# Token numbers from a turned table, a branch moved up with hints, and scatters without an order

## The chip, the cores and the metric

The kernel runs on one core of a Trainium2 chip. A core has a matrix engine (PE, with its weight loads PEld), a vector engine (DVE), an activation engine (ACT), a general engine (POOL, which also issues indirect DMAs), a sync engine (SP, which issues most other DMAs), and 16 DMA engines. Each engine runs its own instruction stream in order; semaphores tie the streams together. The metric is device microseconds of one execution; lower is better.

## The reference, cut to what matters

Three layers follow one another. The first is retention attention over 8 batches, 8 heads, 576 positions and 64 dimensions: scores `q @ k^T / 8`, multiplied by a decay `gamma ** (i - j)` for `i >= j` and 0 otherwise, then multiplied by `v`. Its output is laid out as 4608 tokens of 512 numbers.

The second is a mixture of experts: each token goes to one of 8 experts, the one with the largest gate logit, and becomes `gate_w * (relu(x @ w1[e]) @ w2[e])` with `w1[e]` of 512 x 1024. Which tokens an expert gets is known only while the kernel runs.

The third is a dense layer for all tokens: `h = relu(x @ w_in)` and `(h * h) @ w_out`, with 2048 hidden columns. The output is 4608 rows of 512 numbers in the order of the tokens.

## The kernel before, in words

**Phase 0** computes the attention in 36 tiles of 128 tokens, the gate, and each token's place in a table. The table has 288 columns (36 for each expert) of 128 rows, and holds token numbers: the tokens of one expert fill its columns one after another. It is made by matmuls in one PSUM bank (`tps`), and `tab_out` (line 252) writes it as whole numbers into `tab`, 128 partitions by 288 columns. The token rows lie in DRAM as `xd`.

**Phases 1 and 2** (`phase12`, line 676) run the experts over slots of 512 tokens. The slots in order are `"E"`, then 0 to `NF` = 8; slot `NF` has 256 tokens. Every slot has 8 units `(s, f)`, so the main loop counts `i` from 0 to 79, and slot `NF` is `i` = 72 to 79. In step `i` the code issues `first` of the next unit (12 matmuls, then `hh` on ACT and `hl` on DVE) and `second` of this one (12 matmuls), then splits a piece of a later expert's weights into a high and a low part (`wsplit`: ACT writes the high part, DVE the low one) and loads another from DRAM (`wload`, line 404). Beside it `convs` turns the weights of the third layer into the form that phase 3 wants and stores them in DRAM as `wc`, and `combos` does the same for the first tile's inputs.

A slot's tokens are gathered by `gather` (line 429): POOL copies 4 columns of `tab` into `ix` and fetches the rows of `xd` that they name. At the slot's end `second` stores the results as `yd` (line 847) and the slot's token numbers as `sd` (line 848). The tile `ix` holds a token number in each of 128 partitions, so this store of 2 KB writes 512 single numbers of 4 bytes:

```
sp.dma_start(so.rearrange("(j p) -> p j", p=P), ix[:, :wd // P])
```

If the tokens need more slots than there are, `extra` (line 916) runs them inside `tc.If(ext > x)`, nested for up to 7 more; `ext` is read at run time, and in these inputs the body isn't run. The branch stands in every engine's stream, and behind it each engine waits on its own semaphores. `extras` (line 935) is called at `u == (NF, 4)`, that is `i` = 76.

Four pairs of loads of third-layer weights (`wload2`, line 1022, whose DMAs are of line 1026, 8 in all, 896 KB each) are issued on SP: the pair `(0, 0)` and the pair `(0, 1)` at `i` = 73, the pair `(0, 2)` at `i` = 77, and the pair `(1, 0)` at `i` = 79.

**Phase 3** (`phase3`, line 1101) runs the third layer by 7-product block multiplication over 9 tiles of 512 tokens in 3 passes over the hidden columns. Its first tile needs all 12 loads of the first pass: the 8 above and 4 more of line 1143. The order of its instructions is written by a planner (`Plan`, line 1034): each operation is added with its engines, a guessed duration, keys read and written, and a time to land; `emit` works out due times backwards through the dependencies and then lists the operations by earliest start, ties by due time. In the last pass each tile ends with 4 indirect DMAs on POOL (line 1291), which scatter 128 rows each into `out`, at the token numbers `ixs` that were read back from `sd`. All of them write the key `("out",)`, so the planner, and the waits in the program, put each behind the one before.

Of the kernel before, what the change touches and what calls it, by code (L numbers as in the profile page):

```python
# [9 lines left out]
F32 = mybir.dt.float32  # L10
F32R = mybir.dt.float32r
BF16 = mybir.dt.bfloat16
I32 = mybir.dt.int32
U32 = mybir.dt.uint32
AF = mybir.ActivationFunctionType
ALU = mybir.AluOpType
AX = mybir.AxisListType
# [7 lines left out]
P = 128  # L25
NTILE = NT // P
TS = 512
NF = 8
# [5 lines left out]
KEYS = NE * DMAX  # L34
MAGIC = 12582912.0
IDOFF = float(NT // 2)
# [54 lines left out]
def kernel(ctx, tc, qT, kT, kN, vN, modT, w_gate, mbias, w1, w2, w_in, w_out,  # L91
# [32 lines left out]
    ring = [psX]  # L124

    xd = dram.tile([NT, DM], F32, name="xd")
    yd = dram.tile([DM, NT + TS], F32, name="yd")
    sd = dram.tile([NT + TS], I32, name="sd")
    wc = dram.tile([2, NFP, 2, P, 7 * 256], F32, name="wc")
    pd = dram.tile([9, P, 4 * DM], F32, name="pd")  # L130
    xc = dram.tile([9, 7, P, 4 * 256], F32, name="xc")
# [119 lines left out]

    def tab_out():
        dve.tensor_scalar(out=tab, in0=tps, scalar1=IDOFF, scalar2=None, op0=ALU.add)

    def count(t, name):
        ps = ring[0].tile([P, NE], F32, tag="g", name=name)
# [419 lines left out]
    def phase12():  # L676
        ring[0] = psG
        with ExitStack() as c1:
# [144 lines left out]
            def second(u, cols=range(KD)):  # L823
                s, f = u
                wd = width(s)
                hh, hl = HS.pop(u)
                w = W[s, f // 2][1]
                for c in cols:
                    if f == 0:
                        Y[s, c] = new(psY, [P, TS], F32, f"y{c}", f"y{c}")  # L830
                    cs = slice(c * P, c * P + P)
                    three(Y[s, c][:, :wd], (w[:, 0, f % 2, cs], w[:, 1, f % 2, cs]), (hh, hl), f == 0, f == 7)
                if f == 7:
                    if 0 in cols:
                        YE[s] = new(rp, [P, KD, TS], F32, "raw", "ye")
                    ye = YE[s]
                    for c in cols:
                        act.activation(ye[:, c, :wd], Y[s, c][:, :wd], AF.Copy)
                    if 3 not in cols:
                        return  # L840
                    ix = XG[s][1]
                    if s == "E":
                        yo, so = yd[:, 0:TS], sd[0:TS]
                    else:
                        reg = sp.value_load(slots[0:1, 2, s:s + 1], min_val=0, max_val=NT)
                        yo, so = yd[:, bass.ds(reg, wd)], sd[bass.ds(reg, wd)]
                    sp.dma_start(yo.rearrange("(c p) t -> p c t", p=P), ye[:, :, :wd])
                    sp.dma_start(so.rearrange("(j p) -> p j", p=P), ix[:, :wd // P])

            seq = ["E"] + list(range(NF + 1))  # L850
            us = [(s, f) for s in seq for f in range(8)]
# [62 lines left out]
                    yield  # L914

            def extra(x):
                with tc.If(ext > x):  # L917
                    s_ = NF + 1 + x
                    expert(s_)
                    gather(s_)  # L920
# [41 lines left out]
            for i, u in enumerate(us):  # L962
# [12 lines left out]
                        trans(nx, f - 3)  # L975
                if u == (NF, 7):
                    wload2(1, 0, wp)
                second(u)
                if s == "E" and f == 6:
                    trans(nx, 2)  # L980
# [3 lines left out]
                if i == 0:  # L984
                    for _ in route_a(last):
                        pass
                    next(cs)
                elif i == 1:
                    tb = table()
                    next(tb)  # L990
                    for _ in route_b(last, dve):
                        next(tb)
                elif i == 2:
                    ws(6, 2, 7)
                    tab_out()
                    for _ in range(10):
                        next(tb)
                elif i == 3:
                    for _ in tb:
                        pass  # L1000
                    ws(8, 2, 11)
                else:
                    wl(i + 9)
                    fill(wsg(i + 6, 2 if i < 10 else 1, i + 9), part(cs, 2250))
                    if i >= 68:
                        run(ex, 3)
                    if i == 73:
                        assert next(cs, 0) == 0 and next(ex, 0) == 0
                        wload2(0, 0, cv)
                if u == (NF, 1):  # L1010
                    wload2(0, 1, wp)
                if u == (NF, 4):
                    extras()
                if u == (NF, 5):
                    wload2(0, 2, wp)
                if i == 6:
# [84 lines left out]
    def phase3():  # L1101
        with ExitStack() as c2:
# [10 lines left out]
            xt = sb("xt", [P, 2, 256], F32)  # L1113
            OE = [sb("oe", [P, 4, DM], F32), yr]
            ixs = [sb(f"ix{j}", [P, 4], I32) for j in range(2)]
            BX, BY, BZ = banks[5:7], [banks[7], banks[4]], banks[0]
            BR = {c: banks[1 + "XYZ".index(c)].rearrange("p (b d) -> p b d", b=2) for c in "XYZ"}

# [131 lines left out]
            def hsplit(u, z, h, a, b, kz_):  # L1250
# [5 lines left out]
                                                          in1=h[:, 0, a:b].bitcast(F32), op=ALU.subtract),  # L1256
                         rs + ks[0], ks[1])

            def two(n, x):
                p, t = T3[n]  # L1260
                ends = p == len(PASSES) - 1
# [24 lines left out]
                if x in (4, 3):  # L1286
                    j0 = 2 if x == 4 else 0
                    kk = [("o", v, y) for y in ((4, 7) if x == 4 else (1, 6))]
                    if ends:
                        for j in (j0, j0 + 1):  # L1290
                            plan.add([(POOL_, 1.0)], lambda e, j=j: e.indirect_dma_start(  # L1291
                                out=out[:, :],
                                out_offset=bass.IndirectOffsetOnAxis(ap=ixs[n % 2][:, j:j + 1], axis=0),
                                in_=oe[:, j, :], in_offset=None), kk + [("ix", n % 2)], [("out",)], 4.2)
                    elif T3[n + 1][1] != t:
                        dma(pd[t, :, j0 * DM:j0 * DM + 2 * DM], oe[:, j0:j0 + 2].rearrange("p j d -> p (j d)"),
                            512, kk, [("pd", t, j0)])
# [77 lines left out]
```

## Time and profile before

| what | value |
| --- | --- |
| time, median of 3 runs (lowest to highest) | 1387.73 us (1386.54 to 1390.43) |
| the profiled execution: its time, its span | 1390.15 us, 1387.9 us |
| mean granted TensorE clock | 0.988 of full speed |
| PE busy (share of the span) | 1336.8 us (96%) |
| DVE, ACT, POOL busy | 1023.7, 628.2, 128.9 us |
| DMA | 332.43 MB, mean 240 GB/s |

The profile comes from one execution; all times in it are counted from the start of its span. A busy PE is one that has an instruction in its pipeline. In a view by stretches, `PEclk` is the granted clock of TensorE as a share of full speed and `DMA` the mean busy share of the 16 DMA engines, in which a packet counts from its start to its end, so that waiting packets count too. "Waits" tells which engine and line waited for which.

### The profile page before, as it was taken

How to read it: one execution, taken by the hardware profiler on the slowest of the kernel's cores; microseconds unless marked ns; L12 is line 12 of the kernel's file. 1: busy time of each engine (PE TensorE's matmuls, PEld its weight loads, DVE VectorE, ACT ScalarE, POOL GpSimd, SP SyncE). 2: the span in 40 equal slices, each digit the busy share in tenths (PEclk: the TensorE clock that was granted, in tenths of full speed). 3: DMA queues.
4: the chain of work that ended last, by engine and by line, in shares of the span. 5: the costliest groups of instructions: out<-in, count | busy, mean ns of one | idle time of the engine just before them, and what ended most of it. 6: DMA issues, size and time to landing. Idle time of an engine off the chain costs nothing. (4 is left out here: it accounts for less than half of the span.)

```text
span 1387.9 us, 26914 instructions
## 1 busy us (share of the span) xinstructions
PE 1336.8 (96%) x10640; PEld 1231.3 (89%) x10640; DVE 1023.7 (74%) x2084; ACT 628.2 (45%) x1265; POOL 128.9 (9%) x134
## 2 busy tenths in 40 slices
PE   6999999999999999988899999999999999999995
PEld 6888877888878888877899999999999999999995
DVE  2787867877878778443788888867887777777675
ACT  1444345454444545333566555643444344443442
POOL 3222103110110110000000000000000001111111
PEclk9999999999999999998999999999999999999998
DMA  9988258898898888688645555477799756655541
GB/s 325 392 309 306 81 194 268 264 261 245 280 290 264 235 303 252 175 247 250 264 171 194 204 215 208 181 280 276 284 339 330 280 223 210 211 193 183 175 175 46
DMA packets 143782, 332.43 MB, mean 240 GB/s; under 512 B 20256, under 2 KB 54560, under 8 KB 143648
## 3 DMA queue, kind: packets, MB, share of 16 engines
q1 hardware_dynamic: 135520, 310.06, 66.2%
q0 software_dynamic: 5920, 19.40, 3.9%
q8 instruction: 85, 1.39, 0.4%
q10 hardware_dynamic: 2208, 1.17, 0.3%
q14 instruction: 49, 0.40, 0.1%
HBM read 222.57 MB, written 108.02 MB: 238 GB/s over the span
## 5 line engine op out<-in xcount | busy, mean ns | idle before, releaser
L1153 PE MATMUL bank<-w,h 128*128 128x256 f32 x1008 | 283.4, 281 | 4.9 <-DMA w<-wc 4.9
L1153 PE MATMUL bank<-x,w 128*128 128x256 f32 x1008 | 285.8, 284 | 0.5 <-DVE x L1130 0.5
L1152 PE MATMUL bank<-w,h 128*128 128x256 f32 x1008 | 283.3, 281 | 2.6 <-DVE oe L1130 1.7
L1152 PE MATMUL bank<-x,w 128*128 128x256 f32 x1008 | 285.2, 283 | 0.0
L1154 PE MATMUL bank<-x,w 128*128 128x256 f32 x1008 | 285.1, 283 | 0.0
L1154 PE MATMUL bank<-w,h 128*128 128x256 f32 x1008 | 283.1, 281 | 0.8 <-DVE h L1255 0.7
L1127 ACT ACTIVATE z<-bank 128x256 f32<-128x256 f32 x288 | 109.8, 381 | 256.7 <-PE bank L1154 249.8
L1153 PEld LDWEIGHTS bank<-w,h 128*128 128x128 f32 x1008 | 190.2, 189 | 5.5 <-DMA w<-wc 5.5
L1153 PEld LDWEIGHTS bank<-x,w 128*128 128x128 f32 x1008 | 192.8, 191 | 1.1 <-DVE x L1130 0.7
L1152 PEld LDWEIGHTS bank<-w,h 128*128 128x128 f32 x1008 | 190.7, 189 | 3.5 <-ACT h L1254 2.4
L1154 PEld LDWEIGHTS bank<-x,w 128*128 128x128 f32 x1008 | 193.1, 192 | 0.0
L1152 PEld LDWEIGHTS bank<-x,w 128*128 128x128 f32 x1008 | 192.6, 191 | 0.0
L1154 PEld LDWEIGHTS bank<-w,h 128*128 128x128 f32 x1008 | 190.4, 189 | 1.3 <-DVE h L1255 1.2
L1254 ACT ACTIVATE h<-z 128x512 fp32r<-128x512 f32 (+2 forms) x270 | 159.7, 601 | 66.1 <-DVE z L1130 47.8
L1255 DVE TENSOR_TENSOR h<-z,h 128x512 fp32r<-128x512 f32 (+2 forms) x270 | 169.3, 647 | 7.8 <-ACT h L1254 7.8
L1130 DVE TENSOR_TENSOR z<-z,bank 128x256 f32<-128x256 f32 x216 | 89.2, 416 | 68.9 <-PE bank L1154 57.2
L800 PE MATMUL bank<-hh,wy 128*128 128x512 f32 (+1 forms) x320 | 126.7, 396 | 6.2 <-ACT hh L816 6.2
L800 PE MATMUL bank<-xh,wx 128*128 128x512 f32 (+1 forms) x320 | 123.8, 387 | 3.5 <-PEq L917 3.5
L801 PE MATMUL bank<-hl,wy 128*128 128x512 f32 (+1 forms) x320 | 123.8, 387 | 1.1 <-DVE hl L817 1.1
L801 PE MATMUL bank<-xl,wx 128*128 128x512 f32 (+1 forms) x320 | 123.6, 386 | 1.1 <-DVE xl L756 1.1
L802 PE MATMUL bank<-xh,wx 128*128 128x512 f32 (+1 forms) x320 | 123.5, 386 | 0.0
L802 PE MATMUL bank<-hh,wy 128*128 128x512 f32 (+1 forms) x320 | 123.4, 386 | 0.0
(167 smaller groups left out, 2130.9 us busy)
## 6 DMA issues: line engine op xcount, KB each, us to landing
x<-xc SPq DMA_DIRECT2D x112, 512.0 KB
wr<-w SPq DMA_DIRECT2D x80, 512.0 KB
xc<-x SPq DMA_DIRECT2D x63, 512.0 KB
w<-wc SPq DMA_DIRECT2D x32, 896.0 KB
wc<-cwh SPq DMA_DIRECT2D x16, 896.0 KB
wc<-cwl SPq DMA_DIRECT2D x16, 896.0 KB
pd<-oe SPq DMA_DIRECT2D x24, 512.0 KB
xd<-xs SPq DMA_DIRECT2D x9, 1024.0 KB
```

The source lines that it names most:

```text
L800: pe.matmul(ps, lh, rh, start=first, stop=False)
L801: pe.matmul(ps, lh, rl, start=False, stop=False)
L802: pe.matmul(ps, ll, rh, start=False, stop=last)
L1127: plan.add(a_(c), lambda e: e.activation(o, i, f), r, w)
L1130: plan.add(engs or d_(c), lambda e: e.tensor_tensor(out=o, in0=a, in1=b, op=op), r, w)
L1152: e.matmul(ps[n], lh, rh, start=first and n == 0, stop=False, skip_group_check=True)
L1153: e.matmul(ps[n], lh, rl, start=False, stop=False, skip_group_check=True)
L1154: e.matmul(ps[n], ll, rh, start=False, stop=True, skip_group_check=True)
L1254: plan.add(a_(c), lambda e: e.activation(h[:, 0, a:b], z[:, a + 1:b + 1], AF.Copy), rs, ks[0])
L1255: plan.add(d_(c), lambda e: e.tensor_tensor(out=h[:, 1, a:b], in0=z[:, a + 1:b + 1], in1=h[:, 0, a:b].bitcast(F32), op=ALU.subtract), rs + ...
```

## The change

- After `tab_out`, a new generator `tab_turn` makes a second copy of the table with rows and columns exchanged, and stores it in DRAM as `td`, 288 rows of 128 token numbers: one DVE operation at `i` = 2, and at `i` = 4 three PE transposes, one DVE copy and one DMA on SP.
- The store of a slot's token numbers copies rows of `td` to `sd`, from DRAM to DRAM. Their place is read into a register on SP at each slot's end.
- `extras` is called at `i` = 73, ahead of the loads `(0, 0)` and `(0, 1)`, and at `i` = 71 all five engines get a hint that names the branch.
- Each scatter gets its own key for the planner, its order against other scatters is declared unneeded, and a `memset` of one column on POOL stands before each.

```
+HINTED = [getattr(mybir.EngineType, e) for e in ('PE', 'DVE', 'Activation', 'SP', 'Pool')]
...
+    td = dram.tile([KEYS, P], I32, name="td")
...
+    def tab_turn():
+        tf = s1.tile([P, KEYS], F32, tag="tf", name="tf")
+        ti = s1.tile([KEYS // 3, 3, P], I32, tag="ti", name="ti")
+        dve.tensor_scalar(out=tf, in0=tps, scalar1=IDOFF, scalar2=None, op0=ALU.add)
+        yield
+        ps = ring[0].tile([P, 3, P], F32, tag="g", name="pst3")[:KEYS // 3]
+        for j in range(3):
+            pe.transpose(ps[:, j, :], tf[:, KEYS // 3 * j:KEYS // 3 * (j + 1)], ident)
+        yield
+        dve.tensor_copy(ti, ps)
+        sp.dma_start(td.rearrange("(j k) b -> k j b", j=3), ti)
+        yield
...
-                    ix = XG[s][1]
+                    nt = wd // P
+                    key = sp.value_load(eslot[0:1, 1:2] if s == "E" else slots[0:1, 1, s:s + 1], min_val=0,
+                                        max_val=KEYS - nt)
...
-                    sp.dma_start(so.rearrange("(j p) -> p j", p=P), ix[:, :wd // P])
+                    sp.dma_start(so.rearrange("(j p) -> j p", p=P), td[bass.ds(key, nt), :])
...
-                with tc.If(ext > x):
+                with tc.If(ext > x, label=f"extra{x}"):
...
+                if i == 71:
+                    tc.mark_branch_hint_location("extra0", 0, HINTED)
                 second(u)
...
+                    turn = tab_turn()
+                    next(turn)
...
+                    run(turn, 9)
                     fill(wsg(i + 6, 2 if i < 10 else 1, i + 9), part(cs, 2250))
...
                     if i == 73:
                         assert next(cs, 0) == 0 and next(ex, 0) == 0
+                        extras()
                         wload2(0, 0, cv)
                 if u == (NF, 1):
                     wload2(0, 1, wp)
-                if u == (NF, 4):
-                    extras()
...
+            gap = sb("gap", [P, 1], F32)
...
+            def scatter(e, n, oe, j):
+                at = bass.IndirectOffsetOnAxis(ap=ixs[n % 2][:, j:j + 1], axis=0)
+                e.memset(gap, 0.0)
+                made = e.indirect_dma_start(out=out[:, :], out_offset=at, in_=oe[:, j, :], in_offset=None)
+                tc.declare_no_dep(made.ins, group="rows", reason="a token's row is written once: sd is a permutation")
+                tc.add_to_no_dep_group("rows", made.ins)
...
-                            plan.add([(POOL_, 1.0)], lambda e, j=j: e.indirect_dma_start(
-                                out=out[:, :],
-                                out_offset=bass.IndirectOffsetOnAxis(ap=ixs[n % 2][:, j:j + 1], axis=0),
-                                in_=oe[:, j, :], in_offset=None), kk + [("ix", n % 2)], [("out",)], 4.2)
+                            plan.add([(POOL_, 1.0)], lambda e, j=j: scatter(e, n, oe, j),
+                                     kk + [("ix", n % 2)], [("out", n, j)], 4.2)
```

## Rows read from the trace of the kernel before

**Rows 1.** Stretches of the main phases: length, busy time of each engine (instructions), PEclk, DMA, GB/s.
```profile
225.00:620.00 395.00, 392.95 (x1810) 320.04 (x1811) 296.45 (x371) 187.93 (x263) 34.93 (x34) 1.00 0.86 258
...
1075.00:1365.00 290.00, 288.74 (x2428) 288.16 (x2427) 214.81 (x464) 124.50 (x272) 32.81 (x32) 1.00 0.56 200
```

**Rows 2.** Stretches around the branch and in phase 3's first tile; columns PE, PEld, DVE, ACT, POOL.
```profile
611.70:620.52 8.82, 8.82 (x75) 8.61 (x73) 2.98 (x4) 1.76 (x3) 0.00 (x0) 1.00 1.10 186
620.52:643.22 22.70, 12.26 (x73) 11.70 (x73) 2.74 (x5) 3.19 (x8) 0.00 (x0) 0.70 0.77 267
626.68:638.24 11.56, 7.28 (x31) 6.72 (x31) 2.02 (x4) 0.61 (x2) 0.00 (x0) 0.50 0.57 209
638.24:643.22 4.98, 4.98 (x43) 4.98 (x43) 0.42 (x1) 1.20 (x4) 0.00 (x0) 1.00 1.02 426
659.90:668.47 8.57, 4.87 (x26) 4.46 (x26) 5.56 (x14) 3.26 (x8) 0.00 (x0) 0.80 0.90 360
```

**Rows 3.** ACT from 610 to 640 us: start, us, line, tiles, [idle before <- releaser].
```profile
625.30 1.06 ACT L153 ACTIVATE wy<-wr 128x1024 fp32r<-128x1024 f32 x1 [10.04 <-DMA wr<-w]
```

**Rows 4.** Waits from 612 to 646 us: waiter <- releaser: us, times, longest.
```profile
PE bank L800 <- ACT hh L816: 6.2, 1, 6.2
...
PE bank L800 <- PEq L917: 3.5, 1, 3.5
```

**Rows 5.** DMA issues on SP from 604 to 660 us: start, length, line, tiles, count.
```profile
609.55 0.40 SPq L847 DMA_DIRECT2D yd<-ye  x1
610.18 0.56 SPq L848 DMA_DIRECT2D sd<-ix  x1
611.25 0.75 SPq L404 DMA_DIRECT2D wr<-w  x1
612.05 26.28 SPq L1026 DMA_DIRECT2D w<-wc  x8
```

**Rows 6.** Stretches behind two of the stores of `sd`; the last column is GB/s.
```profile
616.00:620.00 4.00, 4.00 (x36) 4.00 (x35) 0.00 (x0) 0.00 (x0) 0.00 (x0) 1.00 1.04 69
288.00:292.00 4.00, 4.00 (x19) 3.23 (x18) 4.00 (x5) 1.55 (x2) 0.00 (x0) 1.00 0.59 9
```

**Rows 7.** Instructions of the branch, line 917: ns min/median/max, first and last start.
```profile
L917 SPq EVENT_SEMAPHORE  x9: 17/17/17, 627.9 to 636.1; - x9
...
L917 SPq COMPARE_BRANCH  x1: 53/53/53, 615.2 to 615.2; - x1
...
L917 PEldq COMPARE_BRANCH  x1: 6032/6032/6032, 628.1 to 628.1; - x1
```

**Rows 8.** By line, instructions like the added ones: ns min/median/max.
```profile
L1366 POOL MEMSET const-float32-0.0<- x1: 99/99/99, 0.3 to 0.3; 128x1 f32 x1
...
L753 PE MATMUL bank<-ident,xg x152: 271/272/328, 182.3 to 599.1; 128*128 128x128 f32 x152
...
L253 DVE TENSOR_SCALAR tab<-bank x2: 444/446/447, 167.7 to 205.5; 128x288 int32<-128x288 f32 x2
...
L845 SPq TENSOR_LOAD <-slots x9: 277/284/1641, 277.9 to 638.4; - x9
```

**Rows 9.** Waits from 644 to 670 us, phase 3's first tile.
```profile
PE bank L1153 <- DMA w<-wc: 3.3, 2, 1.8
```

**Rows 10.** DVE from 1365 us to the end.
```profile
1375.03 0.69 DVE L1130 TENSOR_TENSOR oe<-oe,bank 128x512 f32<-128x512 f32 x1 [1.47 <-PE bank L1154]
```

**Rows 11.** POOL from 1370 us to the end: start, us, engine, line.
```profile
1373.84 0.97 POOL L1291 DMA_INDIRECT out<-oe,ix  x1 [18.12 <-DVE oe L1130]
...
1383.33 0.97 POOL L1291 DMA_INDIRECT out<-oe,ix  x1 [2.03 <-DMA out<-oe,ix]
```

**Rows 12.** POOL from 261 to 270 us, indirect DMAs that don't wait for one another.
```profile
263.15 0.95 POOL L438 DMA_INDIRECT xg<-xd,ix  x1 [0.30 <-issue]
264.40 0.95 POOL L438 DMA_INDIRECT xg<-xd,ix  x1 [0.30 <-issue]
```

## The prediction

> **What bounds the kernel now.** I read the page's busy times first: PE is busy for 1336.8 of 1387.9 us. A change can therefore gain only where PE stands still or runs at the lower granted clock, or behind its last matmul. Cutting the span into stretches [rows 1] shows where that isn't: 392.95 busy of 395.00 us in the expert phase, 288.74 of 290.00 in phase 3's last pass, both at full clock. It also shows where it is [rows 2]: from 620.52 to 643.22 us PE works 12.26 of 22.70 us, and from 659.90 to 668.47 us it works 4.87 of 8.57. Third, the waits of these stretches and the DMA issues ahead of them name the causes. Last, I read the end on POOL and DVE.
>
> The first hole is a chain. ACT waits 10.0 us for a weight load, `wr`, before it can split it [rows 3], and the `hh` that PE needs stands behind that split in ACT's stream: PE waits 6.2 us [rows 4]. The load was issued at 611.25, right behind the store of `sd` at 610.18 [rows 5]. Behind that store the DMA engines count as fully busy and move 69 GB/s; behind the store of an earlier slot they move 9 GB/s [rows 6]; without one they move 426 [rows 2]. In the earlier slots PE doesn't notice, as [rows 1] shows.
>
> Next comes the branch: PE's COMPARE_BRANCH holds its stream for 6.03 us from 628.1 [rows 7], of which PE shows 3.5 us as idle [rows 4]; the rest lies under matmuls already issued. And from 626.68 to 638.24 us the granted clock is 0.50 of full speed, the level of 1.2 GHz [rows 2], after the 6.2 us of standstill.
>
> **Part 1, the stretch from 620.52 to 643.22 us.** The code has 6 groups of 12 matmuls left there (`second` of steps 76 to 79, `first` of units 78 and 79), 72 in all; the row counts 73, one of them cut by its edge. In the stretch before, 75 take 8.82 us at full clock, 0.1176 us each [rows 2]. So the work takes 8.5 us instead of 22.70: 14.2 us to be had, if the load comes in time and the branch costs nothing.
>
> The load: with 2 KB copied in rows, what stands ahead of `wr` is the store of `yd`, 1 MB, issued at 609.55 [rows 5]. 1.5 MB take 3.5 us at 426 GB/s, and SP issues both later by one more register load. The one there takes 0.28 to 1.64 us [rows 8]; I take 1.2 with its bookkeeping. So `wr` lands at about 616 to 617 us. PE runs dry at 620.52, and between the landing and PE lie a split of 1.06 us [rows 3] and an `hh`, for which I allow 0.6 us with its handing over: about 2 us of cover are left. Without that cover each us late costs one. The nine other register loads on SP lie beside weight loads that are three pieces ahead; the expert phase has 2 us of idle PE in 395, so they cost nothing unless that cover goes; then up to 1.8 us each.
>
> The branch: no row shows a hinted one. By the code the hint stands 60 matmuls ahead of the branch on PE, at 0.1176 us each 7 us or more; the unhinted fetch took 6.03 us under load [rows 7], so I take it as hidden. Behind the branch PE waits for its own last matmul, and I take 0.4 us for that bubble. Bounds: 0, and the 3.5 us seen, with a lower clock behind it. The hint instruction itself shows in no row; on PE I take 0.15 us, between 0 and the 1.64 of the longest register load. Part 1: -14.2 + 0.4 + 0.15 = -13.65 us, between -14.2 and -9.
>
> **Part 2, the first tile of phase 3.** From 659.90 to 668.47 us 26 matmuls run, 3.1 us of work at 0.1176, so 5.5 us are lost, to `w<-wc` loads [rows 9] and to the clock behind them (0.80 on the mean [rows 2]). PE now gets there earlier, so what is late next is these loads. Today SP issues four, meets the branch at 615.2, gets no further instruction before 627.9, and is through its waits at 636.1 [rows 7]. The change puts the branch ahead of all twelve loads. SP then waits, before the first, for its own DMAs in flight, by the sum above until 617 us. From 618 on, twelve loads of 0.917 MB and 0.5 MB of `yd` take 27 us at 426 GB/s, to about 645. Phase 3 starts at 620.5 + 8.5 + 0.55 = 629.6. The first pair of loads is in at 622.5. The wait that ended at 668.47 lies, in PE's work, 16.7 us (643.22 to 659.90) and 25 matmuls, 2.9 us, behind the start: at 649. So the last load has some 4 us to spare. Most of the 5.5 us go; I take -4.0, since part of that spare time could be eaten by SP's wait at the branch. Bounds: -5.5 and 0.
>
> **Part 3, the end.** PE's last matmuls end at 1375.0, and the last add ends at 1375.03 + 0.69 = 1375.72 [rows 10]. The four scatters start at 1373.84 and then about every 3 us, the last at 1383.33 [rows 11], each behind the landing of the one before. Indirect DMAs without such a wait start 1.25 us apart [rows 12]; with a `memset` of 0.1 us [rows 8] I take 1.4. The last then starts at 1373.84 + 4.2 = 1378.0, later than its data, and 5.3 us sooner. Four in flight share the DMA engines, so I give 0.3 us back: -5.0. Bounds: at 1.25 us -5.7; and -1, if the memset serialises POOL and the landings stretch. The 32 earlier scatters hide under the last pass of [rows 1].
>
> **Part 4, what is added early.** Three transposes on PE: 0.27 us each, 0.8 in all [rows 8], less where they overlap; PE has no idle time to hide them: +0.6 (0 to 1.5, with a wait for their bank). DVE gets one read of 288 columns, 0.45 us [rows 8], and a copy of 384, about 0.5; DVE is busy for 296 of 395 us in that phase [rows 1], so they hide; at worst +1. SP waits for that copy before it stores `td`, with the next weight load queued behind it, about a us against three pieces of lead. The `ix` copies on POOL no longer wait for the stores of `sd`, but the gathers behind them wait for PE's transposes anyway: nothing.
>
> **Sum.** -13.65 - 4.0 - 5.0 + 0.6 = -22.05 us against the profiled execution's 1390.15 us, which gives 1368.1. That execution stands 2.4 us above the median of the three runs; on the median, 1387.73 - 22.05 = 1365.7, so **1366 us**.
>
> **Rivals.**
>
> *The hints bring nothing.* Each engine then pays the fetch at the new place. On PE 6.03 us less the 2.5 already hidden now is 3.5, and a lower clock behind a standstill of 3.5 us: the 31 matmuls of [rows 2] at 0.50 would take 3.6 us more than at full speed, for half as long a stretch 1.5. That is 5 us: 1371. If SP also sits at the branch as it does now, 12.7 us from 615.2 to 627.9, the loads end at 656 instead of 645, and part 2's gain goes too: 1375. For it: no trace here shows a hint at work. Against it: SP's 12.7 us fall into the slow stretch behind `sd`, which goes. The Trainium skill, "Runtime: NRT & Kernel Launch", section "Instruction fetch mechanics", says that prefetch is purely sequential and that a taken branch to a target outside the window stalls for a fetch. By that rule this rival is the outcome; the trace agrees as to the stall without a hint (6.03 us) and can't say what a hint does.
>
> *The loads stay late though the hints work*, since the first now waits for SP's DMAs to land: part 2 brings 0, 1370.
>
> *The slow DMA stretch isn't made by the 4-byte writes,* so the change doesn't do what it says: parts 1 and 2 keep only the branch, 3.5 us and a part of the clock; with the end's 5, 1378. Against it: the low rate stands behind the stores of `sd` in an early slot and in a late one [rows 6].
>
> *Slower: the planner writes a worse last pass.* Without the common key the scatters' due times move later by up to 5.2 us (its 1.0 and 4.2) for each that followed, and with them those of the adds on DVE that feed them. DVE is at 74% in the last pass [rows 1]; an add that comes late keeps its PSUM bank, and PE waits for it. It decides from 22 us over nine tiles, 2.5 us a tile. At 3 us a tile the time is 1366 + 27 = 1393. Against it: a bank's adds also get due times from the matmuls that reuse the bank, and these don't move.
>
> **How the numbers follow.** The forecast, 1361 to 1369, has a chance of 0.55; no help from the hints (1371 to 1375) 0.17; late loads alone 0.10; a slow stretch that stays 0.05; the planner 0.08 (0.05 of it slower than before); some loss that I don't see, 0.05, of which 0.02 end slower. A measurement of this kernel can tell about 0.3%, 4 us, from no change. Faster by more: all but the planner's slower part, an equal part near no change, and some of the unseen: 0.88. Within: 0.05. Slower: 0.07. The range goes from 1360, where every part meets its better bound (-14.2 - 5.5 - 5.7 is -25.4, and a little more from gaps I left alone), to 1377, which takes in the hints' and the loads' failure together and leaves out about 0.17.
>
> **What would show it.** Right: no ACT wait for `wr` near 615 us; more than 300 GB/s behind each store of `sd`; a short COMPARE_BRANCH on PE; phase 3's first matmul near 630 us; no `w<-wc` wait in its first 20 us; the scatters at the end less than 2 us apart. Wrong: a COMPARE_BRANCH of some us on PE or SP; PE idle in the last pass for more than the 1.3 us it is now; a new wait of SP ahead of the twelve loads that runs past 620 us.

## The result, and the profile after

The changed kernel takes 1374.95 us (median of 4 runs, 1372.95 to 1377.90) against 1387.13 us for the kernel before in the same session: a ratio of 0.9911, interval [0.9885, 0.9936]. It is faster by 0.9%, and the time lies in the range; but 12.2 us were gained, and 22 were forecast. The profiled executions differ by 14.7 us (1390.15 and 1375.41). The 2.5 us between these two figures come from the chosen executions: the one of before stands 3.0 us above the median here, the one of after 0.5.

I cut both traces at the same instructions: TensorE's first and last transpose of a gathered slot, its first matmul of phase 3, the starts of its second tile, its last pass and its last tile, TensorE's end, and the end of the span. The tiles of phase 3 overlap, so their starts are counted, 84 matmuls for each 256 hidden columns: 252 to a tile in the first and the last pass, 168 in the second. Lengths in us:

| stage | before | after | change | forecast |
| --- | --- | --- | --- | --- |
| start to the first transpose of a slot | 182.30 | 183.11 | +0.8 | 0 |
| to the last transpose (the expert phase) | 416.81 | 418.97 | +2.2 | +0.6 (part 4) |
| to phase 3 (the branch) | 44.11 | 31.98 | -12.1 | -13.65 (part 1) |
| first tile of phase 3 | 35.85 | 32.46 | -3.4 | -4.0 (part 2) |
| rest of the first two passes, and the last pass's first tile | 454.64 | 455.07 | +0.4 | 0 |
| seven tiles of the last pass | 209.21 | 211.80 | +2.6 | 0 |
| its last tile | 32.07 | 32.92 | +0.9 | 0 |
| behind TensorE's end | 12.94 | 7.33 | -5.6 | -5.0 (part 3) |
| span | 1387.9 | 1373.6 | -14.3 | -22.05 |

So what was forecast to go did go, nearly all of it: 21.1 us of 22.65. What was given back, 6.8 us, is what the forecast had put at 0.6.

The stretches of the trace after, in the columns of [rows 1, 2] (length, then busy us and instructions of PE, PEld, DVE, ACT, POOL; PEclk, DMA, GB/s). The first answers to the branch, the second to the first tile, the third to the last pass. The fourth and the fifth are the stretches of [rows 6]. They begin 1.5 us behind the issue of an early slot's store of `sd` and of a late one; in the kernel before, where the stores went out earlier, it is 4.9 and 5.8 us. The last stretch runs from the first issue of a load for phase 3 to the end of TensorE's last wait for one:

```profile
602.07:634.05 31.98, 29.26 (x218) 27.75 (x218) 16.24 (x25) 14.09 (x28) 0.00 (x0) 1.00 0.88 321
634.05:666.51 32.46, 30.48 (x254) 30.08 (x253) 25.72 (x54) 20.16 (x44) 0.10 (x1) 1.00 0.89 337
1121.58:1333.38 211.80, 210.72 (x1766) 209.50 (x1765) 151.22 (x323) 89.14 (x210) 30.64 (x56) 1.00 0.56 192
...
288.00:292.00 4.00, 4.00 (x18) 3.21 (x18) 3.96 (x6) 2.50 (x3) 0.00 (x0) 1.00 0.83 282
...
616.00:620.00 4.00, 2.34 (x19) 2.13 (x19) 1.48 (x2) 0.75 (x1) 0.00 (x0) 1.00 0.95 317
...
622.63:655.91 33.28, 31.30 (x260) 30.90 (x258) 18.83 (x42) 16.49 (x39) 0.10 (x1) 1.00 0.98 373
```

The granted clock is 1.00 where [rows 2] show 0.70 and 0.80, and behind the stores of `sd` the DMA engines move 282 and 317 GB/s where [rows 6] show 9 and 69.

The DMA issues on SP, after (answers to [rows 5]: start, length, line, tiles, count):

```profile
613.81 0.41 SPq L864 DMA_DIRECT2D yd<-ye  x1
614.48 0.62 SPq L865 DMA_DIRECT2D sd<-td  x1
615.39 1.12 SPq L419 DMA_DIRECT2D wr<-w  x1
622.63 4.36 SPq L1047 DMA_DIRECT2D w<-wc  x8
```

The instructions of the branch, after (answers to [rows 7]; ns min/median/max, first and last start):

```profile
L934 SPq EVENT_SEMAPHORE  x9: 17/17/17, 617.1 to 622.6; - x9
...
L934 PEldq COMPARE_BRANCH  x1: 402/402/402, 614.6 to 614.6; - x1
...
L934 SPq COMPARE_BRANCH  x1: 73/73/73, 616.6 to 616.6; - x1
L934 DVEq COMPARE_BRANCH  x1: 90/90/90, 616.8 to 616.8; - x1
L934 DVEq EVENT_SEMAPHORE  x1: 21/21/21, 618.0 to 618.0; - x1
```

TensorE's branch takes 0.40 us where it took 6.03. SP is through its nine waits at 622.6 us, not 636.1. Its first load for phase 3 goes out at 622.63, and phase 3 begins at 634.06, 11.4 us later; the prediction had 618 and 629.6, 11.6 us apart. ScalarE's split of the late `wr`, after (answer to [rows 3]):

```profile
622.43 1.06 ACT L155 ACTIVATE wy<-wr 128x1024 fp32r<-128x1024 f32 x1 [1.90 <-SPq L934]
```

From the issue of that load to its split 7.0 us pass (615.39 to 622.43), where it was 14.0 (611.25 to 625.30, [rows 3, 5]). Of ScalarE's 10.0 us of waiting 1.9 are left.

TensorE's waits from 602 to 667 us, after (answers to [rows 4, 9]: waiter, releaser, us, times, longest):

```profile
PE bank L1175 <- DMA w<-wc: 2.0, 2, 1.3
PE bank L815 <- DVEq L934: 1.7, 1, 1.7
```

The second of the two waits for loads, with its end (TensorE's timeline):

```profile
655.91 0.38 PE L1175 MATMUL bank<-w,h 128*128 128x256 f32 x1 [1.34 <-DMA w<-wc]
```

No wait for `wr` stands ahead of TensorE any more; of 6.2 and 3.5 us at the branch 1.7 are left, and of 3.3 in the first tile 2.0. The scatters at the end, after (answers to [rows 11]):

```profile
1365.17 0.97 POOL L1284 DMA_INDIRECT out<-oe,ix  x1 [24.31 <-DVE oe L1152]
...
1368.99 0.97 POOL L1284 DMA_INDIRECT out<-oe,ix  x1 [0.19 <-issue]
```

Four scatters lie 3.82 us apart from first to last, 1.27 each, where [rows 11] have 9.49. Two costs show that I had not seen coming. The first is in the first slot. TensorE's waits from 220 to 232 us:

```profile
PE bank L768 <- DMA xg<-xd,ix: 2.7, 1, 2.7
```

TensorE waits for gathered rows. GpSimd's timeline ahead of it (start, us, engine, line, operation, tiles, [idle before <- releaser]), and then VectorE's:

```profile
216.99 0.95 POOL L453 DMA_INDIRECT xg<-xd,ix  x1 [0.31 <-issue]
218.24 4.39 POOL L453 DMA_INDIRECT xg<-xd,ix  x1 [0.30 <-issue]
```

```profile
217.22 0.56 DVE L266 CAST ti<-bank 96x384 int32<-96x384 f32 x1 [1.77 <-PE bank L264]
217.70 1.21 DVE L156 TENSOR_TENSOR wx<-wr,wx 128x1024 fp32r<-128x1024 f32 x1
218.83 0.69 DVE L721 TENSOR_SCALAR cwk<-craw 128x1024 uint32<-128x1024 uint32 x1
```

VectorE waits 1.77 us for the added transposes, and from 217.22 us on it runs without a pause. Beside that, the gather's fourth DMA takes 4.39 us; the third took 0.95.

The second cost is in the last pass. TensorE's waits from 1121.58 to 1366.30 us, after:

```profile
PE bank L1174 <- DVE oe L1152: 1.6, 2, 0.8
PE bank L1174 <- ACT z L1149: 1.1, 6, 0.2
```

The waits for `z` are new: in the same stretch of before TensorE has only that for `oe`, 1.5 us. They lie in the seven tiles, and are 1.1 of the 2.6 us by which these grew. The rest lies in matmuls that count as busy for longer: 210.72 us for 1766 of them, against the 209.20 that e5 below shows for as many.

### The profile page after: what moved, and what is told of

Its sections match the earlier page's. It is cut to its first block, busy times and chain, and to the rows that moved or that the text cites. A ratio compares the mean times of both kernels' runs of the same rounds, so it can differ in the third digit from the quotient of the medians.

```text
span 1373.6 us, 26947 instructions
## 1 busy us (share of the span) xinstructions
PE 1334.8 (97%) x10643; PEld 1228.3 (89%) x10643; DVE 1022.4 (74%) x2077; ACT 627.4 (46%) x1283; POOL 131.0 (10%) x170
## 4 chain that ended last, share of the span: by engine, by line
PE 47%; DMA 3%; DVE 2%; ACT 0%; issue 0%; POOL 0%; SPq 0%; POOLq 0%
PE bank L1176 16%; PE bank L1174 16%; PE bank L1175 16%; DMA w<-wc 3%; DVE z L1152 1%; DVE h L1277 0%; DVE z L1160 0%; ACT h L1276 0%; POOL out L1284 0%; SPq L1047 0%; DVE oe L1152 0%; ACT z L1149 0%; DVE x L1152 0%; DVE yr L1152 0%; POOLq L1398 0%
```

## The experiments

Medians are of each kernel's runs, ratios those to the kernel before in the same session. Stages are cut as above: A the expert phase, B from the last transpose to phase 3, C the first tile, D seven tiles of the last pass, E its last tile, F behind TensorE's end. Each row of stages is one execution. How far such rows repeat, kernels with the same code in a stage show: B and C within 0.3 and 0.6 us over after, e5, e6, e7 and e13, but 2.1 and 1.2 us apart between before and e3, which both have the slow stretch.

| kernel | median us | ratio, interval | A | B | C | D | E | F |
| --- | --- | --- | --- | --- | --- | --- | --- | --- |
| before | 1387.13 | | 416.81 | 44.11 | 35.85 | 209.21 | 32.07 | 12.94 |
| after | 1374.95 | 0.9911 [0.9885, 0.9936] | 418.97 | 31.98 | 32.46 | 211.80 | 32.92 | 7.33 |
| e1 only copied numbers | 1380.04 | 0.9942 [0.9922, 0.9962] | 419.10 | 37.40 | 31.44 | 209.21 | 31.93 | 12.98 |
| e2 only moved, hinted branch | 1385.20 | 0.9987 [0.9977, 0.9996] | 416.54 | 36.00 | 38.67 | 209.21 | 31.99 | 13.31 |
| e3 only independent scatters | 1385.99 | 0.9989 [0.9979, 0.9998] | 416.21 | 42.00 | 34.66 | 213.09 | 32.93 | 7.50 |
| e4 after, no hints | 1380.35 | 0.9960 [0.9946, 0.9973] | 416.09 | 40.55 | 31.45 | 213.05 | 32.96 | 7.30 |
| e5 after, one planner key | 1370.89 | 0.9887 [0.9863, 0.9910] | 419.07 | 31.98 | 32.04 | 209.21 | 31.99 | 7.33 |
| e6 after, table later | 1373.55 | 0.9900 [0.9876, 0.9924] | 416.82 | 31.68 | 32.64 | 213.95 | 33.15 | 7.32 |
| e7 = e5 and e6 | 1368.69 | 0.9869 [0.9845, 0.9894] | 415.98 | 31.68 | 32.42 | 209.21 | 31.90 | 7.35 |
| e8 after, branch at its old place | 1376.12 | 0.9923 [0.9898, 0.9947] | 418.60 | 30.79 | 34.00 | 213.02 | 32.96 | 7.36 |
| e10 = e7 without the branch | 1365.88 | 0.9844 [0.9828, 0.9861] | 416.72 | 30.62 | 31.45 | 209.21 | 31.99 | 7.33 |
| e12 = e7, only TensorE hinted | 1375.17 | 0.9902 [0.9885, 0.9919] | 416.20 | 37.92 | 31.48 | 209.21 | 32.01 | 7.33 |
| e13 = e5, copy on ScalarE | 1370.27 | 0.9878 [0.9847, 0.9910] | 417.11 | 31.67 | 32.68 | 209.21 | 32.00 | 7.33 |

**e1 to e3: each part alone, on the kernel before.**

```
e1: + tab_turn and its calls
    - sp.dma_start(so.rearrange("(j p) -> p j", p=P), ix[:, :wd // P])
    + sp.dma_start(so.rearrange("(j p) -> j p", p=P), td[bass.ds(key, nt), :])
e2: + mark_branch_hint_location at i == 71, extras() at i == 73
e3: + scatter(), its key ("out", n, j) and its memset
```

> The row copy of the token numbers alone (branch at i = 76 without hints, scatters with their order). Theory: the 4-byte writes of sd made the slow DMA stretch, so the wait of ACT for the last wr load and PE's 6.2 us go, with the lower clock behind them; the branch still costs PE some 3 us or more. From the end of the PE gap near 600 us to the first matmul of phase 3: 36 to 38 us (before 44.3, after 32.1); last pass and end as before; time about 1379. The gap of PE near 226 us is 2 us or more, as after. Rival, the slow stretch has another cause: 44 us and about 1387.

> The moved and hinted branch alone (4-byte store of sd, scatters with their order). Theory: the COMPARE_BRANCH on PE takes under 1 us instead of 6.0, but ACT still waits for wr some 10 us and PE some 6; the same stretch takes 39 to 41 us; the gap near 226 us is 0.5 us as before; time about 1383. Rival, the load was late because of the four loads issued behind it and not because of sd: these now stand behind the branch, ACT does not wait, 33 us and about 1376.

> The scatters alone (own keys for the planner, no order in the program). Theory: the end shortens by 5.6 us as after, and the planner's other order costs 0.4 us a tile in the last pass, 3.3 us in all: time 1385. Rival, the 3.3 us of the last pass come from the scatters running at once with other transfers or from the earlier parts: here they show only if the order is the cause in a kernel without the other parts; without them the time is 1381.5.

By medians the three gain 7.4, 2.3 and 1.5 us, 11.2 together, against 12.2 for all at once. With an interval of 5.3 to 10.8 us for e1 alone, a loss between them of a few us can't be told. Stages B and C say what each does. e1, which still has the slow branch, takes them from 79.96 us to 68.84: the 4-byte writes were the largest cost here. e2 takes them to 74.67. Its branch is fast on TensorE, but the loads come late, and TensorE waits 2.3 us for an `hh`. Forecast were 6 us of this, behind ScalarE's wait for `wr`, and 39 to 41 us for B; B came to 36.0, and the cause is another. ScalarE's own event behind the branch comes 8.9 us after the branch, though it was hinted, and `hh` follows it; the split of `wr` comes only after that. In the changed kernel the same event takes 4.5 us, without cost for TensorE, and in e7 1.3. So on ScalarE the hint doesn't always help; why, no run shows. TensorE's and ScalarE's branch and TensorE's waits (from 600 to 675 us) in e2, then TensorE's two in e1 (601 to 670):

```profile
L932 PEldq COMPARE_BRANCH  x1: 397/397/397, 612.4 to 612.4; - x1
...
L932 ACTq COMPARE_BRANCH  x1: 76/76/76, 613.1 to 613.1; - x1
...
L932 ACTq EVENT_SEMAPHORE  x1: 17/17/17, 622.0 to 622.0; - x1
```

```profile
PE bank L1170 <- DMA w<-wc: 3.3, 2, 1.7
PE bank L1169 <- DMA w<-wc: 2.3, 1, 2.3
PE bank L815 <- ACT hh L831: 2.3, 1, 2.3
```

```profile
L934 PEldq COMPARE_BRANCH  x1: 6492/6492/6492, 623.0 to 623.0; - x1
```

```profile
PE bank L815 <- PEq L934: 5.1, 1, 5.1
```

e3 gains 5.4 us in F and gives 4.7 back in D and E; that is why the dropped order was worth 1.5 us by itself (0.3 to 2.9 by its interval) and not 5.

**e4: the changed kernel without the hints.**

```
-                if i == 71:
-                    tc.mark_branch_hint_location("extra0", 0, HINTED)
```

> The changed kernel without the hint line. Theory: the hints hide the fetch, so without them PE's COMPARE_BRANCH takes 4 to 6 us and PE stands still for 3 to 4.5, with a lower clock behind it; time 1379 to 1381. Rival, the fetch was long only because the DMA engines were slowed behind sd: then it takes 1 to 2 us and the time stays within 1 us of 1375.

The branch is slow again, at its new place. From its lines of the branch and its waits (598 to 670 us):

```profile
L934 PEldq COMPARE_BRANCH  x1: 6212/6212/6212, 610.8 to 610.8; - x1
```

```profile
PE bank L815 <- issue: 7.7, 1, 7.7
```

TensorE stands 7.7 us, more than the 3 to 4.5 expected, and B is 8.57 us longer than in the changed kernel; C is 1.01 shorter, as the loads have caught up by then. The hints are worth 7.56 us over B and C here. The rival fell for TensorE, whose unhinted branch takes 5.91 us in e3 and 6.03 in the kernel before, in the slow stretch, and 6.21 and 6.49 in e4 and e1 without it. For SP it has a point: from its unhinted branch to its first event 12.7 and 10.1 us pass in the slow stretch (before, e3), and 5.0 to 5.3 without it (e1, e4, e12); with the hint it is 0.5.

**e5: one planner key for all scatters, their issue still independent.**

```
-                                     kk + [("ix", n % 2)], [("out", n, j)], 4.2)
+                                     kk + [("ix", n % 2)], [("out",)], 4.2)
```

> The changed kernel, but all last-pass scatters keep one key in the planner, as in the kernel before, while their issue stays independent. Theory (the keys of their own changed the planner's order of the last pass, and this order costs): seven tiles of the last pass in 209.2 us as before, not 211.8; its last tile 32.0, not 32.9; tail after the last matmul 7.3 to 7.7; in all 3 to 4 us less than the changed kernel, median about 1371. Rival (the longer last pass comes from the scatters' own traffic, which now lies closer together): seven tiles stay at 211.5 to 213, median 1375. Rival 2 (the tail's gain came from the planner's order, not from the dropped wait): tail back at 12.9, median 1376 or more.

The theory holds: D and E are back at 209.21 and 31.99 us, F stays at 7.33, and the median falls by 4 us. Its last pass, columns as above:

```profile
1120.47:1329.67 209.20, 209.20 (x1766) 209.20 (x1765) 152.85 (x329) 89.67 (x196) 30.38 (x56) 1.00 0.57 194
```

TensorE is busy without a break, with as many scatters and 194 GB/s, where the changed kernel has 192. The longer pass came from the order that the planner wrote with keys of their own, not from the traffic. Over five kernels with those keys (after, e3, e4, e6, e8) D lies between 211.80 and 213.95; over all eight with the one key (before, e1, e2, e5, e7, e10, e12, e13) it is 209.21.

**e6 and e13: the turned table later, and its copy on another engine.**

```
e6:  -                    run(turn, 9)
     +                    if i == 5:
     +                        run(turn, 9)
e13: -        dve.tensor_copy(ti, ps)
     +        act.activation(ti, ps, AF.Copy)
```

> The changed kernel, but the transposes, the copy and the write of the turned table come one step of the program later (at i = 5, not i = 4). Theory (the added work on VectorE holds up GpSimd's fourth gather of the first slot): TensorE's pause of 2.67 us near 226 us is gone, the stretch from the first expert transpose to the last is 416.5 us and not 419.0, median about 1373. Rival (the pause is chance, or comes with the table wherever it stands): the stretch stays at 419, median 1375.

> The version with one planner key and the table at its place in the changed kernel (i = 4), but the copy of the turned table out of PSUM runs on ScalarE and not on VectorE. Theory (VectorE waits for the transposes, then runs without a pause, and GpSimd's gather of the first slot stands 4.4 us beside that): VectorE no longer waits 1.8 us for the transposes, the long indirect DMA of the first slot shrinks below 2.5 us, TensorE's pause near 225 us is at most 0.7 us and the stretch from the first expert transpose to the last about 417 us, not 419.1. Rival (the pause comes from the transposes on TensorE, or from anything else that the table brings at this place): the pause stays at 2 to 2.7 us and the stretch at 419.

Both take the pause away: A falls from 418.97 us to 416.82 in e6, and from e5's 419.07 to 417.11 in e13. The same fourth DMA of the first slot in e13's timeline of GpSimd, TensorE's waits from 200 to 240 us there, and the DMA in e6:

```profile
217.36 0.95 POOL L453 DMA_INDIRECT xg<-xd,ix  x1 [0.30 <-issue]
```

```profile
PE bank L768 <- DVE hl L832: 0.5, 1, 0.5
```

```profile
216.44 1.54 POOL L453 DMA_INDIRECT xg<-xd,ix  x1 [0.31 <-issue]
```

In e13 the transposes stay where they were, so by themselves they are not the cause. By e13, one execution, VectorE's added wait and copy are needed for the pause; but they don't bring it each time. Of the five kernels with the table at `i` = 4 and its copy on VectorE, four have 418.60 to 419.10 us in A (after, e1, e5, e8), and e4 has 416.09. GpSimd in e4:

```profile
216.23 0.95 POOL L453 DMA_INDIRECT xg<-xd,ix  x1 [0.30 <-issue]
217.18 3.73 POOL L450 COPY ix<-tab 128x4 int32 x1
```

VectorE's copy and the run behind it begin at 216.30 us there, beside the start of the fourth DMA, which takes 0.95 us; the long one is GpSimd's next operation, a copy for the slot after, and TensorE doesn't wait. In the other four the fourth DMA begins 1.0 us behind the copy, and takes 4.4 us. So GpSimd is held up each time, and a microsecond decides whether TensorE pays.

By median e6 is 1.4 us ahead of the changed kernel and e13 0.6 ahead of e5; the runs overlap, and neither is told from the spread. The next kernel shows the gain in the time: e7 is 2.2 us below e5 in the same session, and their runs don't overlap.

**e7: both mends.**

> Both edits together (one planner key for the scatters, the turned table one step later). Both theories right: about 5 us less than the changed kernel, median 1369.5. Only the planner's: 1371 to 1372. Only the table's: 1373. Neither: 1375.

1368.69 us, all its runs (1367.75 to 1370.29) below all of the changed kernel's. This is the best version with the whole function: 18.4 us below the kernel before, 6.3 below the changed kernel. It was a little better than the 1369.5 expected.

**e8: the branch back at its old place, hinted.**

```
                     if i == 73:
                         assert next(cs, 0) == 0 and next(ex, 0) == 0
-                        extras()
                         wload2(0, 0, cv)
...
+                if u == (NF, 4):
+                    extras()
```

> The changed kernel, but the branch stands at its old place (the last slot's fifth step), with the hints. Theory (the hint pays for the code fetch wherever the branch stands, and the new place only moves the loads of phase 3's first tile): TensorE's branch 0.4 us as in the changed kernel; pauses at the branch 1 to 3 us; the first tile of phase 3 31.4 to 33 us; time from the last transpose to phase 3 30 to 33 us; median 1374 to 1376, the same as the changed kernel. Rival (the place is what pays: behind the branch the queue of loads waits for its own last writes): from the last transpose to phase 3 and the first tile together 4 us or more longer than the changed kernel's 64.4, median 1379 or more.

B and C together take 64.79 us; the changed kernel has 64.44. With hints the place makes no difference that these two executions show, and the medians, 1.2 us apart, overlap in their runs. Without hints it does, and to the worse: 68.84 at the old place (e1), 72.00 at the new (e4). So the hints did part 1's second half, and moving the branch added nothing to it. What the old place costs is the first tile, which waits 1.8 us for a load. That tile came out 1 us above what was expected. SP's nine semaphore events behind the branch in e8, then in e7:

```profile
L934 SPq EVENT_SEMAPHORE  x9: 17/17/17, 616.8 to 629.1; - x9
```

```profile
L934 SPq EVENT_SEMAPHORE  x9: 17/17/17, 612.8 to 618.0; - x9
```

In e8 four of the loads were issued ahead of the branch, from 614.00 us, and SP is through its waits 12.3 us after they began; in e7 it takes 5.2. Those waits are for SP's own DMAs in flight, and nothing is issued meanwhile: by the semaphores of the trace of the changed kernel, the last of them end with the landings of `yd`, `sd` and `wr`, at 621.2, 621.4 and 622.4 us.

**e10: what the hinted branch still costs** (e7 with the blocks for overflowing experts left out).

```
-                if i == 71:
-                    tc.mark_branch_hint_location("extra0", 0, HINTED)
...
-                        extras()
```

> The kernel of the last experiment but one (one planner key, table one step later) with the branch and its hint left out altogether: the blocks for overflowing experts, which these inputs do not need, are gone from the program. What is lost against it is the price that the hinted branch still has. Theory (behind a branch each engine waits until the others have passed, and the queue of loads waits until its own last writes have landed, 5.3 us; the first tile of phase 3 then lacks weights twice): TensorE's pause of 1.36 us at the branch gone, the first load for phase 3 issued at about 612.5 and not 618.0, the first tile 31.4 and not 32.4, from the last transpose to phase 3 30 to 30.5 and not 31.7; together 2 to 3 us, median 1366 to 1367. Rival (the first tile's pauses come from the order and the volume of its loads, not from the drain): the first tile stays at 32.4, median 1367.5 or more, only the 1.36 us gone.

The theory holds, in full for C and nearly for B. SP's loads, and TensorE's waits from 597 to 660 us, in e10:

```profile
609.40 1.11 SPq L419 DMA_DIRECT2D wr<-w  x1
610.57 6.25 SPq L1045 DMA_DIRECT2D w<-wc  x8
```

```profile
PE bank L816 <- DVE xl L771: 1.1, 1, 1.1
PE bank L1174 <- DVE h L1275: 0.6, 1, 0.6
PE bank L816 <- DVE hl L832: 0.3, 1, 0.3
```

The loads follow `wr` at once. C is 31.45 us, as in every kernel whose loads are in time (e1, e4, e12), and B and C together are 2.03 us shorter than in e7. The median gains 2.8, of which the stages explain those 2.03; the rest isn't told apart from the spread.

**e12: only TensorE hinted** (on e7).

```
-                    tc.mark_branch_hint_location("extra0", 0, HINTED)
+                    tc.mark_branch_hint_location("extra0", 0, HINTED[:1])
```

> The same kernel with one planner key and the table one step later, but only TensorE is hinted; VectorE, ScalarE, SyncE and GpSimd come to the branch without. Theory (each engine fetches its own code behind the branch, and TensorE behind it waits for the others): TensorE's own branch stays at 0.4 us, but it then waits for VectorE or ScalarE at the branch for 4 to 7 us in place of 1.36; from the last transpose to phase 3 36 to 40 us, not 31.7; median 1373 to 1377. Rival (TensorE's fetch alone is what mattered, the others have slack): at most 33 us, median 1369 to 1370.

TensorE passes its branch in 0.40 us and then waits for VectorE. The branch lines of both, TensorE's waits from 601 to 671 us, and the stretch at the lower clock:

```profile
L934 PEldq COMPARE_BRANCH  x1: 397/397/397, 613.4 to 613.4; - x1
...
L934 DVEq COMPARE_BRANCH  x1: 72/72/72, 615.5 to 615.5; - x1
...
L934 DVEq EVENT_SEMAPHORE  x1: 21/21/21, 621.2 to 621.2; - x1
```

```profile
PE bank L815 <- DVEq L934: 6.1, 1, 6.1
```

```profile
617.91:624.74 6.83, 3.45 (x16) 3.45 (x17) 0.01 (x1) 0.43 (x2) 0.00 (x0) 0.50 0.44 145
```

VectorE's COMPARE_BRANCH lasts 72 ns, and its semaphore event comes 5.7 us after it; in the changed kernel, hinted, it came 1.2 us after, when the operation that VectorE had in work (616.78 to 618.00 us) was done. So on VectorE the missing hint shows as a hole behind the branch, while on TensorE it shows in the branch's own duration. Within the 6.1 us of waiting the granted clock falls to 0.50, the level of 1.2 GHz, and stays there for 6.83 us. The median is 6.5 us above e7's. Over B and C the hint on TensorE alone brings 2.6 us (72.00 in e4, 69.40 here), the other four 5.3 (64.10 in e7). Which of the four counts was not tried one by one. SP can't be it: its waits end 6.0 us behind its branch in e12 and in the changed kernel alike, since they last until `wr` has landed.

## Why the prediction was right, and where its size was off

That the time lies in the range is in part luck. The forecast proper, 1361 to 1369, missed, and the range went up to 1377 to take in the failure of the hints and the loads together. That is not what happened: the hints worked on TensorE, and most of what moved the time up are two losses elsewhere, 3.4 us in the last pass and 2.2 in the first slot, put at 0 and 0.6 in the sum.

**Part 1, -13.65, came to -12.1.** Both causes were the right ones. The DMA rate behind `sd` is back, and of ScalarE's 10.0 us 1.9 are left, for which TensorE doesn't wait. Without the standstill the granted clock stays at 1.00 from 183 to 1371 us. The term that was too small is "Behind the branch PE waits for its own last matmul, and I take 0.4 us": it is 1.7 us, and the wait is for VectorE, which reaches the branch at 616.8, behind its own queue, and signals at 618.0, when its last operation is done. That a branch makes engines wait for one another I had not priced, though [rows 7] show SP's nine semaphore events.

**Part 2, -4.0, came to -3.4.** SP's wait was foreseen rightly. Its loads start at 622.63 us and not at 618, but phase 3 starts as much later: the loads go out 11.4 us ahead of it, where the prediction had 11.6. (3.0 us of the shift come from the stages before.) What failed is the size of "27 us at 426 GB/s": from the first issue to the end of TensorE's last wait for a load 33.3 us pass, 346 GB/s for the same 11.5 MB; the engines moved 373 in all, since the loads were not alone. So the "4 us to spare" were used up, and two waits of 2.0 us together are left. e7 has the same 33.3 us. e10 shows the other side: without the drain the loads go out 16.3 us ahead of phase 3, and none is waited for.

**Part 3, -5.0, came to -5.6.** 1.27 us a scatter against the 1.4 taken; the landings didn't stretch. The part that failed is its last sentence, "The 32 earlier scatters hide under the last pass". The scatters do hide, but the new keys changed the planner's order, at +3.4 us over eight tiles (e5). This was the rival "the planner writes a worse last pass", and its mechanism came true in part: the waits that are new are for a bank that comes free late, but it is a copy by ScalarE (`z`) that frees it, not an add by VectorE, and 1.5 us of the seven tiles' 2.6 show as no wait at all. Its price was set at 2.5 to 3 us a tile; it was 0.37 to 0.85. I had treated it as a thing that happens in full or not at all, and put nothing of it into the sum.

**Part 4, +0.6, came to +2.2.** The three transposes themselves cost next to nothing: with the table one step later A is 416.82 us, as before. What failed is "the gathers behind them wait for PE's transposes anyway: nothing". It holds for slots with lead; the first slot's gather has none, since its token numbers are made just then. By GpSimd's and VectorE's rows the gather's fourth DMA stood beside an unbroken run of VectorE, and it doesn't in e13, where VectorE idles 3.21 us up to 217.80, into the fourth DMA. In e4 the DMA begins just ahead of the run, and isn't held up. The Trainium skill, "SBUF — State Buffer", section "SBUF: two separate sides", says that GpSimd is locked out of the port pair that the two share, and can't write the descriptors of its DMAs, while VectorE runs an operation in a 2-port mode. The trace agrees as to the delay (4.39 us in place of 0.95); that the port is its cause, and which operation of the run would hold it, no run here shows.

**The rivals.** *The hints bring nothing* fell: on TensorE 0.40 us with a hint, 5.91 to 6.49 without (before, e1, e3, e4). The Trainium skill, "Runtime: NRT & Kernel Launch", section "Instruction fetch mechanics", describes sequential prefetch and a stall at a taken branch; e4 agrees as to the stall, and on TensorE, VectorE and SP the hint takes it away; on ScalarE not always (e2). Had the rival been right, the time would have been e4's 1380.35; I had put it at 1371 to 1375, too low by the planner's order (4.7 us over D and E in e4) and by the standstill, put at 5 us and worth 7.56 over B and C. *Loads stay late* came true in small part: they are waited for, but part 2 still brought 3.4 us. *The slow stretch isn't from the 4-byte writes* fell by e1.

**What stays open.** The 0.8 us ahead of the expert phase are not explained; over the kernels here this stage runs from 179.57 us (e10) to 185.34 (e3), though none of the edits touches it. The clock has a part in that: its mean is 1.00 in e10 from 20.9 us to the stage's end, and 0.96 in e3 from 14.6. In the middle of phase 3, 0.4 us longer, TensorE waits 2.4 us for loads of weights after, and 1.5 before. Nor is it explained why D differs by up to 2.15 us between kernels with the same planner's order.

## What to carry to other kernels

A branch that stands in every engine's stream is a meeting point: look at what each engine still has queued and at every DMA in flight ahead of it, and hint it for all engines (on TensorE alone it brought 2.6 us here, on the other four together 5.3). When an order is dropped from a program whose schedule a planner writes, drop it in the issue and keep it in the planner's keys, and read the pass that the planner writes anew before counting the gain. For what is added "where there is slack", look for the one iteration that has none: here it was the first slot.

## What the runs showed of the hardware that I had not expected

- A store of 2 KB as 512 numbers of 4 bytes held up the rest of the DMA traffic for microseconds: 9 and 69 GB/s behind it [rows 6], 282 and 317 with the same 2 KB in rows. The load of 512 KB issued behind the late one was ready to be split 14.0 us after its issue, and 7.0 us with the rows.
- Behind a branch SP issues nothing until its DMAs in flight have landed: 5.2 us in e7, and 12.3 in e8, where four loads of 896 KB were among them.
- An unhinted branch holds TensorE for 5.9 to 6.5 us (before, e1, e3, e4) and VectorE for 4.5 us more than a hinted one (5.7 in e12 against 1.2), and TensorE waits for VectorE behind it; around the end of the 6.1 us of standstill in e12 the clock was at half for 6.83 us.
- A hint doesn't always help ScalarE: its event came 8.9 us behind a hinted branch in e2 and 4.5 in the changed kernel, 1.3 in e7.
- What GpSimd begins beside an unbroken run of VectorE can take much longer: a DMA in the changed kernel (4.39 us in place of 0.95), a copy in e4 (3.73, where the same copy takes 0.2 to 1.2 us in the other kernels).
